# Sums of squares of two weight matrices moved from ScalarE to TensorE, and all low bits of their decoding to ScalarE

## The chip, the cores and the metric

The kernel runs on one core of a Trainium2 chip. The metric is the device time in microseconds. A core has TensorE (PE in the profile; its weight loads are PEld), VectorE (DVE), ScalarE (ACT), GpSimd (POOL) and SyncE (SP), which here only issues DMAs. Every engine works through a queue of its own in order, and engines wait for each other by semaphores.

## The reference

Three parts follow each other: an attention with two softmaxes, a block with a two-dimensional Fourier transform and two large products, and a block with token shift and three products. Inputs are fp32; q, k and v are 8x8x576x64, so that there are 8 batches of 576 tokens with 512 channels.

```python
q_s = softmax(q, axis=-1); k_s = softmax(k, axis=2)
x = q_s @ (k_s.T @ v)                       # per batch and head
mixed = real(fft(fft(x, axis=1), axis=2))
u = x + mixed
un = (u - mean(u)) / sqrt(var(u) + 1e-6)
x = u + relu(un @ w_ch1) @ w_ch2            # 512x2048 and 2048x512
xk, xr = mixes of x with the token before it
out = sigmoid(xr @ w_r) * (relu(xk @ w_k) ** 2 @ w_v)
```

The softmaxes are written here as one word each. The weights of the change are `w_ch1` (w1) and `w_ch2` (w2).

## The kernel before

**Products.** A factor is kept as two fp16 parts, a rounded one and the rest, and a product is three products of parts. The main loop goes over nine blocks of up to 512 tokens. For each block and each of 16 chunks f, `mm1` (L1104) makes 128 hidden channels out of w1, and `mm2` (L1127), two chunks behind, adds their share of w2's result into four banks of PSUM. Between these products `side()` puts the next steps of attention, Fourier transform and norm of later batches, and later the work of the third part, whose products are in L1165, L1218 and L1230.

**The front.** Before the main loop can begin, batch 0 must be through attention, transform and norm, and the weights must be ready. Three generators produce this: `front_x` (attention of each batch: maxima L337 to L349, softmaxes L360 to L376, products L381, transposes L416, results L436), `front_y` (transform: sums and differences L473 to L488, first products L517, second products L537, then the norm with the sums L647) and `front_z` (the weights). `beside_first` takes one step of x or y and, by the rate RATE, 0.4 steps of z, each pinned behind the newest instructions of VectorE and ScalarE. What is left of z follows behind batch 0's norm.

**The weights.** A weight arrives as 32-bit words in pairs, of which the upper word has all but three bits of the value. The 16 chunks of w1 and the 16 of w2 are handled two at a time, in 16 pairs of 128x1024 values, 1 MB of DMA each. Six pairs are loaded ahead; the load of pair k+4 is issued by SP once the high join of pair k has released its buffer (L228, L229). Step k of `front_z` does three things:

- `low_parts(k)`: VectorE shifts the upper words (L168). The low bits are then taken in one of two ways. With `own`, VectorE joins them with a shift (L170). Without it, ScalarE stores them into the low half of the raw upper word (L172), and the next operation brings them along.
- `high_parts(k-1)`: VectorE joins the top bits of pair k-1 (L174), and without `own` the stored low bits too. This waits for L172 of that pair.
- `squares(k-2)`: ScalarE squares all values of pair k-2 and adds them up by row (L234), in an instruction with a read-out of the sum behind it.

`own` is true for even k, so eight pairs go either way. After the last pair of w1 and the last of w2, `scales(w)` adds the eight sums (L243), adds over the partitions with a product by ones (L245), and works out a power of two (L246 to L253). `split(w, c)` then makes the two fp16 parts of each chunk, h on ScalarE (L260) and the rest on VectorE (L261), in place: chunk k is written where chunk k-1 was, so that each split waits for the one before it. The main loop starts with six chunks split, and the other 26 follow beside its first block.

**Warming products.** `warm` (L451) puts products into the front whose result nobody reads, in banks of the tag "h". This tag has two banks, which `mm1` uses later.

The low bits' two ways are in L169 to L172:

```python
if own:
    join(out=x, in0=lo, scalar=29, in1=x, op0=ALU.logical_shift_right, op1=ALU.bitwise_or)
else:
    nc.scalar.activation(out=raw.bitcast(U16)[..., 2], in_=lo, func=AF.Copy, scale=0.9975 * 2.0 ** -29, bias=-0.49)
```

Of the kernel before, what the change touches and what calls it, by code (L numbers as in the profile page):

```python
# [8 lines left out]
F32 = mybir.dt.float32  # L9
F32R = mybir.dt.float32r  # L10
F16 = mybir.dt.float16
BF16 = mybir.dt.bfloat16
U32 = mybir.dt.uint32
U16 = mybir.dt.uint16
AF = mybir.ActivationFunctionType
ALU = mybir.AluOpType
AX = mybir.AxisListType
# [11 lines left out]
POOL_K = ()  # L29
BEHIND_X = {(1, 1): 6}  # L30
RATE = 0.4
OWN = 0
AHEAD_W = 6
FIRST = 1.0
HOLD = {(2, 0): "c"}
# [12 lines left out]
def net(ctx, tc, q, k, v, w1, w2, mu_k, mu_r, w_k, w_v, w_r, ce_d, se_d, cs_d, ss_d, alt_d, id_d, out):  # L48
    nc = tc.nc
# [13 lines left out]
    def bank(tag, bufs, shape=(128, 512)):  # L63
        return ps.tile(list(shape), F32, tag=tag, name=tag, bufs=bufs)
# [3 lines left out]
    def aside(first, strand):  # L68


        turn_of[0] += 1
        if not first:
            return bank(f"side{strand if 'b' in marks or done_block[0] >= 0 else turn_of[0] % 2}", 1)
        x = turn_of[0] % 6
        return bank(f"side{x // 3}", 1) if x in (0, 3) else bank(f"acc{(1, 2, 4, 5).index(x)}", 1)

    mm = nc.tensor.matmul
# [14 lines left out]
    big = main.enter_context(tc.tile_pool(name="big", bufs=1, side="right"))  # L92
# [17 lines left out]
    wr = big.tile([128, len(order) + 1, 512], U32, name="wr", tag="w")  # L110
    wf = wr.bitcast(F16)
    onesr = big.tile([128, 128], F32R, name="onesr")
    ones = onesr.bitcast(F32)
    amax = big.tile([128, 2, 8], F32, name="amax")
    wsc = big.tile([128, 8], F32, name="wsc")

    ident = fc.tile([128, 128], F32, name="ident")
# [45 lines left out]
    def assemble(raw, x, part=None, own=False):  # L163

        hi, lo = raw[..., 1], raw[..., 0]
        join = nc.vector.scalar_tensor_tensor
        if part != 1:
            nc.vector.tensor_scalar(out=x, in0=hi, scalar1=3, scalar2=0x3FFFFFFF, op0=ALU.logical_shift_left, op1=ALU.bitwise_and)  # L168
# [4 lines that stand above are left out]
        if part != 0:  # L173
            join(out=x, in0=hi, scalar=0xC0000000 if own else 0xC0000007, in1=x, op0=ALU.bitwise_and, op1=ALU.bitwise_or)  # L174
# [6 lines left out]
    pairs = [(w, c) for w in range(2) for c in range(0, 16, 2)]  # L181
    raws = {}
# [17 lines left out]
    def load_pair(k):  # L200

        if k >= len(pairs):
            return
        if k == 0:
            raws["places"] = word_places()
        w, c = pairs[k]
        raw = raws[k] = next(raws["places"]).rearrange("p (c n w) -> p c n w", c=2, w=2)
        for x in range(2):
            z = c + x
            if w == 0:  # L210
                src = w1.bitcast(U32)[128 * (z % 4):128 * (z % 4) + 128, 1024 * (z // 4):1024 * (z // 4) + 1024]
            else:
                src = w2.bitcast(U32)[128 * z:128 * z + 128, :]
            nc.sync.dma_start(out=raw[:, x].rearrange("p n w -> p (n w)"), in_=src)

    def words_at(w, c):
        a, b = place[w, c] + 1, place[w, c + 1] + 1
        return wr[:, a:b + 1:b - a]

    def low_parts(k):  # L220

        if k < len(pairs):
            assemble(raws[k], words_at(*pairs[k]), 0, k % 2 == OWN)

    def high_parts(k):
        if 0 <= k < len(pairs):
            assemble(raws.pop(k), words_at(*pairs[k]), 1, k % 2 == OWN)
            if k + 4 >= AHEAD_W:  # L228
                load_pair(k + 4)  # L229

    def squares(w, c):

        dump = wr[:, 0].bitcast(BF16).rearrange("p (c n) -> p c n", c=2)
        nc.scalar.activation(out=dump, in_=words_at(w, c).bitcast(F32), func=AF.Square, accum_out=amax[:, w, c // 2:c // 2 + 1])  # L234

    def scales(w):


        ts = nc.vector.tensor_scalar
        m = wsc[:, 3 * w:3 * w + 1]  # L240
        inv = wsc[:, 3 * w + 1:3 * w + 2]
        mi, ii = m.bitcast(U32), inv.bitcast(U32)
        nc.vector.tensor_reduce(out=m, in_=amax[:, w, :], axis=AX.X, op=ALU.add)  # L243
        pt = aside(False, 0)[:, 0:1]
        mm(out=pt, lhsT=one, rhs=m, start=True, stop=True)  # L245
        ts(out=inv, in0=pt, scalar1=2.0 ** -120, scalar2=None, op0=ALU.max)  # L246
        ts(out=mi, in0=ii, scalar1=1, scalar2=0x3F800000, op0=ALU.logical_shift_right, op1=ALU.bitwise_and)
        ts(out=ii, in0=mi, scalar1=0x7F800000, scalar2=None, op0=ALU.bitwise_xor)

        ts(out=inv, in0=inv, scalar1=(2.0 ** -55, 2.0 ** -51)[w], scalar2=None, op0=ALU.mult)  # L250
        ts(out=m, in0=m, scalar1=(2.0 ** 54, 2.0 ** 50)[w], scalar2=None, op0=ALU.mult)
        if w == 1:
            nc.vector.tensor_tensor(out=wsc[:, 6:7], in0=wsc[:, 0:1], in1=m, op=ALU.mult)  # L253
# [190 lines left out]
    def warm(b, x, src):  # L444

        if b == 0:
            pt = bank("h", 2)
            if len(src.shape) > 2:
                src = src.rearrange(("p a b -> p (a b)", "p a b c -> p (a b c)")[len(src.shape) - 3])
            for _ in range(x):  # L450
                mm(out=pt[:, 0:128], lhsT=ones, rhs=src[:, 0:128], start=True, stop=True)  # L451
# [5 lines left out]
    def transform(b):  # L457
# [11 lines left out]
        if b in (0, 1, 2):  # L469

            for t in range(4):
                for e, op in ((0, ALU.add), (1, ALU.subtract)):
                    tt(out=eo[:, e, t, 1:289], in0=u[:, t, 1:289], in1=u[:, t, S - 1:HALF - 1:-1], op=op)  # L473
                if t == 0 and b == 0:
                    warm(0, 8, eo[:, 0, 0, 1:129])
                if t == 2:
                    nc.scalar.activation(out=x6[0:1, 0:289], in_=eo[0:1, 0, 2, 0:289], func=AF.Copy)
                    tt(out=x6[32:33, 0:289], in0=eo[0:1, 0, 2, 0:289], in1=x6[0:1, 0:289].bitcast(F32), op=ALU.subtract)
                yield 0
            nc.scalar.activation(out=eo[0:1, :, 2, 0:289], in_=eo[0:1, :, 3, 0:289], func=AF.Copy)  # L480
            nc.vector.memset(eo[0:1, 0, 3, 0:289], 0.0)
            for e, op in ((0, ALU.add), (1, ALU.subtract)):
                for g in range(2):
                    tt(out=eo[:, e, g, 0:289], in0=eo[:, e, g, 0:289], in1=eo[:, e, 3 - g, 0:289], op=op)
                    ma = nc.scalar.activation(out=eh[:, e, g, 0:289], in_=eo[:, e, g, 0:289], func=AF.Copy)
                    warm(b, 1, eo[:, e, g, 1:129])
                for g in range(2):
                    mv = tt(out=el[:, e, g, 0:289], in0=eo[:, e, g, 0:289], in1=eh[:, e, g, 0:289].bitcast(F32), op=ALU.subtract)  # L488
# [223 lines left out]
    def last_weights():  # L712
# [35 lines left out]
        def words_of(q):  # L748


            def squares(a, x):
                hw = wp.tile([128, 256], BF16, tag="hw", name="hw", bufs=1)
                nc.scalar.activation(out=hw, in_=x.bitcast(F32), func=AF.Square, accum_out=am[:, q, a:a + 1])

            before = None
            for a, (src, t, c, x) in enumerate(chunks(q)):
                decode(load_weight(wp, src, t, c, RAW), x)
                if before:
                    squares(*before)
                before = a, x  # L760
                yield 0
            squares(*before)
            yield 0
# [200 lines left out]
    def front_z():  # L964
        for k in range(len(pairs) + 2):
            if k < len(pairs):
                low_parts(k)
            high_parts(k - 1)
            if k >= 2:
                squares(*pairs[k - 2])  # L970
            yield 0
            if k - 2 in (7, 15):
                scales((k - 2) // 8)
                yield 0
# [178 lines left out]
    words = big.tile([128, 31, 512], F32, tag="w", name="last")  # L1153
# [221 lines left out]
def build(inputs):  # L1375
    import concourse.bacc as bacc

    nc = bacc.Bacc("TRN2", target_bir_lowering=False, num_devices=1, dynamic_dma_scratch_size=1024)
    arrays, args = {}, []
    for name, a in [*_laid_out(inputs).items(), *_constants().items()]:  # L1380
        arrays[f"in_{name}_dram"] = a
        args.append(nc.dram_tensor(f"in_{name}_dram", a.shape, mybir.dt.from_np(a.dtype), kind="ExternalInput").ap())
    b, _, s, _ = inputs["q"].shape
    args.append(nc.dram_tensor("out_0_dram", (b * s, DM), F32, kind="ExternalOutput").ap())
    with tile.TileContext(nc, schedule_with_timeline_sim=True) as tc:
        net(tc, *args)
    return nc, arrays
# [9 lines left out]
```

## Time and profile before

| | us |
|---|---|
| median of 3 runs | 1457.01 |
| lowest and highest | 1456.41, 1457.19 |
| the profiled execution | 1457.53 |
| its span, first to last instruction | 1455.8 |
| busy: TensorE, its weight loads | 1408.9, 883.1 |
| busy: VectorE, ScalarE, GpSimd | 992.0, 687.4, 26.3 |

The span is shorter than the execution, as the launch and the end lie around it. Busy times are of one profiled execution. Matmuls overlap in TensorE's pipeline and their ends are modelled, so the time that one takes up is better read from the distance between starts than from its duration. The granted clock (PEclk) is the share of 2.4 GHz that TensorE was given; its lower level is 1.2 GHz. A chain of waits is followed back from the last instruction: at each step to what released it, or to the instruction ahead of it on its engine.

### The profile page before, as it was taken

The page shows a single profiled execution, that of the slowest core. Times are in us where ns is not written, and L with a number is a line of the kernel's source. Part 1 is how long each engine was busy: PE and PEld are TensorE (multiplying, and loading weights), DVE is VectorE, ACT ScalarE, POOL GpSimd, SP SyncE. Part 2 cuts the span into 40 slices and gives each one's busy share as a digit, 9 for nine tenths or more (in the row PEclk, how much of TensorE's full clock was granted, in tenths as well). Part 3 has the DMA queues.
Part 4 walks back from the last instruction along what each step waited for, and adds up shares of the span by engine and source line. Part 5 has one row for each costly group of instructions (what it writes and reads, how often), then busy time and mean ns, then how long its engine had stood idle before and what let it go on. Part 6 is the DMA issues. An engine that isn't in the chain of part 4 may idle for free.

```text
span 1455.8 us, 21047 instructions
## 1 busy us (share of the span) xinstructions
PE 1408.9 (97%) x8519; PEld 883.1 (61%) x8519; DVE 992.0 (68%) x1804; ACT 687.4 (47%) x1233; POOL 26.3 (2%) x41
## 2 busy tenths in 40 slices
PE   4679999999999999999999999999999999999998
PEld 3568988886556556556555444445666666666665
DVE  8988686595683774753533476784999788875643
ACT  6776544453342433432322266573766555654422
POOL 1001000000000000000000000000000000000000
PEclk8699999999999999999999999999999999999999
DMA  9830013112011020110011032301011011100001
GB/s 376 297 124 2 18 42 108 54 58 72 17 52 64 27 71 35 52 46 1 0 59 38 15 115 74 116 23 58 30 59 59 22 38 59 52 8 30 29 17 42
DMA packets 38301, 89.47 MB, mean 61 GB/s; under 512 B 5147, under 2 KB 11580, under 8 KB 38204
## 3 DMA queue, kind: packets, MB, share of 16 engines
q1 hardware_dynamic: 37052, 85.30, 16.7%
q0 software_dynamic: 1152, 2.83, 0.6%
q8 instruction: 66, 1.08, 0.3%
q14 instruction: 31, 0.25, 0.1%
HBM read 69.25 MB, written 18.87 MB: 61 GB/s over the span
## 4 chain that ended last, share of the span: by engine, by line
PE 92%; DVE 4%; ACT 2%; issue 1%; DMA 0%; ACTq 0%; DVEq 0%
PE acc L1127 25%; PE h L1104 25%; PE acc L1230 13%; PE h L1165 11%; PE side L1218 6%; PE side L537 2%; PE side L517 2%; PE side L436 2%; PE side L381 1%; PE side L416 1%; DVE wr L174 1%; ACT wr L234 0%; DVE wr L261 0%; PE side L382 0%; ACT u L172 0%
## 5 line engine op out<-in xcount | busy, mean ns | idle before, releaser
L1104 PE MATMUL h<-unh,wr 128*128 128x512 f16 (+1 forms) x1408 | 380.0, 341 | 2.3 <-ACT wr L260 1.4
L1127 PE MATMUL acc<-hh,wr 128*128 128x512 f16 (+1 forms) x1408 | 368.6, 341 | 0.0
L1104 PEld LDWEIGHTS <-wr 128*128 128x128 f16 x2112 | 201.8, 98 | 165.5 <-issue 3.9
L1127 PEld LDWEIGHTS <-wr 128*128 128x128 f16 x2112 | 201.6, 98 | 159.9 <-issue 2.7
L1104 PE MATMUL h<-unl,wr 128*128 128x512 f16 (+1 forms) x704 | 239.3, 341 | 0.0
L1127 PE MATMUL acc<-hl,wr 128*128 128x512 f16 (+1 forms) x704 | 220.0, 341 | 0.0
L1230 PE MATMUL acc<-ring,last 128*128 128x512 f16 x864 | 201.2, 379 | 0.2 <-DVE last L1261 0.2
L1110 DVE SCALAR_TENSOR_TENSOR hl<-h,hh 128x512 f16<-128x512 f32 x144 | 99.1, 688 | 136.0 <-ACT hh L1109 135.2
L1109 ACT ACTIVATE hh<-h 128x512 f16<-128x512 f32 x144 | 85.7, 595 | 170.6 <-PE h L1104 170.1
L1230 PEld LDWEIGHTS <-last 128*128 128x128 f16 x864 | 84.0, 98 | 86.5 <-DVE last L1261 0.7
L1165 PEld LDWEIGHTS <-wkh 128*128 128x128 f16 x1008 | 98.5, 98 | 34.1
L1259 ACT ACTIVATE last<-last,pw 128x512 f32<-128x512 f32 x72 | 51.5, 717 | 106.9 <-DVE last L1258 106.3
L1218 PE MATMUL side<-ring,x 128*128 128x512 f16 x432 | 101.1, 379 | 0.0
L1180 DVE TENSOR_TENSOR last<-h,last 128x512 f32<-128x512 f32 x90 | 61.8, 687 | 49.9 <-PE h L1165 49.8
L1165 PE MATMUL h<-x,wkh 128*128 128x256 f16 x560 | 95.7, 273 | 0.0
L1165 PE MATMUL h<-x,wkl 128*128 128x256 f16 x280 | 76.3, 273 | 0.0
L1165 PE MATMUL h<-last,wkh 128*128 128x256 f16 x448 | 76.1, 273 | 0.0
L1218 PEld LDWEIGHTS <-x 128*128 128x128 f16 x432 | 42.3, 98 | 42.5
L1261 DVE TENSOR_TENSOR last<-last 128x512 f16<-128x512 f32 x72 | 49.5, 687 | 22.1 <-ACT last L1260 21.7
L1165 PE MATMUL h<-last,wkl 128*128 128x256 f16 x224 | 61.1, 273 | 0.0
L894 ACT ACTIVATE aa<-y,ms 128x512 f32<-128x512 f32 x72 | 48.0, 712 | 17.5 <-DVE x L902 12.2
L409 ACT ACTIVATE qT<-side 128x512 fp32r<-128x512 f32 (+3 forms) x44 | 37.0, 840 | 38.3 <-PE side L416 27.7
(358 smaller groups left out, 2087.1 us busy)
## 6 DMA issues: line engine op xcount, KB each, us to landing
vt<-in_v_dram SPq DMA_DIRECT2D x16, 650.0 KB, 5.4
kt<-in_k_dram SPq DMA_DIRECT2D x16, 576.0 KB, 3.9
qt<-in_q_dram SPq DMA_DIRECT2D x16, 576.0 KB, 3.8
out_dram<-oo SPq DMA_DIRECT2D x36, 256.0 KB, 2.0
y<-yT SPq DMA_DIRECT2D x8, 1026.0 KB, 5.3
u<-in_w_dram SPq DMA_DIRECT2D x16, 512.0 KB, 6.2
words<-in_w_dram SPq DMA_DIRECT2D x10, 512.0 KB, 9.9
raw<-in_w_k_dram SPq DMA_DIRECT2D x16, 256.0 KB, 3.6
```

Of the source, the lines that this page charges most:

```text
L409: nc.scalar.activation(out=dst(qT), in_=src, func=AF.Copy)
L894: nc.scalar.activation(out=a, in_=y[:, t, 0:n], func=AF.Copy, scale=mu[:, w, 1, t:t + 1])
L1104: mm(out=pt[:, o:o + m], lhsT=a, rhs=c[:, t, o:o + m], start=(t == z == 0), stop=(t == 3 and z == 2))
L1109: ma = nc.scalar.activation(out=hh[:, 0:n], in_=pt[:, 0:n], func=AF.Relu)
L1110: mv = nc.vector.scalar_tensor_tensor(out=hl[:, 0:n], in0=pt[:, 0:n], scalar=0.0, in1=hh[:, 0:n], op0=ALU.max, op1=ALU.subtract)
L1127: mm(out=acc[x][:, o:o + m], lhsT=a, rhs=c[:, o:o + m], start=(f == z == o == 0), stop=(f == NF - 1 and z == 2), skip_group_check=(i < 2))
L1165: mm(out=pt[:, 256 * x:256 * x + 256], lhsT=c[:, u, 128 * x:128 * x + 128], rhs=d[:, u], start=(fresh and x == u == z == 0), stop=(last an ...
L1180: nc.vector.tensor_tensor(out=out, in0=view(pt), in1=addend, op=ALU.add)
L1218: mm(out=pt, lhsT=a[:, v, u, c, o:o + 128], rhs=w[:, t, :], start=(t == y == 0), stop=(t == 3 and y == 2))
L1230: mm(out=acc[x], lhsT=a[:, 128 * x:128 * x + 128], rhs=c[:, f, :], start=(f == z == 0), stop=(f == 7 and z == 2))
L1259: nc.scalar.activation(out=o, in_=o, func=AF.Square, scale=W["pw"][:, 10 + g:11 + g])
L1261: nc.vector.tensor_tensor(out=l2, in0=o, in1=h2, op=ALU.subtract)
```

## The change

`OWN` becomes empty, so that no pair is `own`: ScalarE stores the low bits of all 16 pairs, and VectorE's low joins in the front are gone. The decoding of the third part's weights doesn't use OWN and stays as it is. `squares` leaves ScalarE: it takes the upper 16 bits of each value as bf16, and for each 128 columns multiplies them on TensorE with themselves, eight products for each pair, adding all 64 of a matrix into a 128x128 corner of one "h" bank. On the diagonal stand the sums of squares of the columns. `scales` multiplies this corner by the identity and adds by row. `warm` keeps one bank, where it took the next of two each time, since the sums hold the other.

```diff
-OWN = 0
+OWN = ()
...
-    amax = big.tile([128, 2, 8], F32, name="amax")
...
-            assemble(raws[k], words_at(*pairs[k]), 0, k % 2 == OWN)
+            assemble(raws[k], words_at(*pairs[k]), 0, k in OWN)
...
-            assemble(raws.pop(k), words_at(*pairs[k]), 1, k % 2 == OWN)
+            assemble(raws.pop(k), words_at(*pairs[k]), 1, k in OWN)
...
     def squares(w, c):
 
-        dump = wr[:, 0].bitcast(BF16).rearrange("p (c n) -> p c n", c=2)
-        nc.scalar.activation(out=dump, in_=words_at(w, c).bitcast(F32), func=AF.Square, accum_out=amax[:, w, c // 2:c // 2 + 1])
+        if "gram" not in raws:
+            raws["gram"] = bank("h", 2)
+        words = words_at(w, c).bitcast(BF16).rearrange("p c (n h) -> p c n h", h=2)[..., 1]
+        for x in range(2):
+            for g in range(0, 512, 128):
+                z = words[:, x, g:g + 128]
+                mm(out=raws["gram"][:, 128 * w:128 * w + 128], lhsT=z, rhs=z, start=(c + x + g == 0), stop=(c + x == 15 and g == 384))
...
-        nc.vector.tensor_reduce(out=m, in_=amax[:, w, :], axis=AX.X, op=ALU.add)
+        dg = wr[:, 0, 128 * w:128 * w + 128].bitcast(F32)
+        nc.vector.tensor_tensor(out=dg, in0=raws["gram"][:, 128 * w:128 * w + 128], in1=ident, op=ALU.mult)
+        nc.vector.tensor_reduce(out=m, in_=dg, axis=AX.X, op=ALU.add)
...
         if b == 0:
-            pt = bank("h", 2)
+            if "idle" not in raws:
+                raws["idle"] = bank("h", 2)
+            pt = raws["idle"]
```

## Rows read from the trace of the kernel before

**Rows 1.** The page's 40 slices of the span: busy tenths, and granted clock (PEclk).

```profile
PE   4679999999999999999999999999999999999998
...
DVE  8988686595683774753533476784999788875643
...
PEclk8699999999999999999999999999999999999999
```

**Rows 2.** Busy us (instructions) by stretch: PE, PEld, DVE, ACT, POOL; clock, DMA share, GB/s.

```profile
17.90:98.10 80.20, 53.86 (x269) 45.25 (x268) 74.48 (x125) 64.29 (x110) 4.71 (x8) 0.77 0.70 262
20.00:45.00 25.00, 14.03 (x53) 11.29 (x54) 24.03 (x38) 22.44 (x41) 4.71 (x8) 0.65 1.07 406
45.00:70.00 25.00, 15.40 (x72) 12.32 (x71) 23.49 (x46) 18.53 (x34) 0.00 (x0) 0.70 0.71 250
70.00:98.00 28.00, 23.60 (x140) 21.07 (x139) 24.79 (x40) 21.35 (x35) 0.00 (x0) 0.91 0.34 133
98.00:130.00 32.00, 27.35 (x225) 22.68 (x223) 30.07 (x53) 19.43 (x34) 4.52 (x2) 1.00 0.17 59
130.00:1452.00 1322.00, 1321.26 (x8003) 809.87 (x8003) 874.31 (x1606) 598.45 (x1084) 16.23 (x24) 1.00 0.13 46
```

**Rows 3.** The chain of waits from 17 to 98 us, by line.

```profile
by line: issue 15.2%; DVE wr L174 9.4%; ACT wr L234 7.8%; ACT u L172 6.6%; ACT words L172 6.2%; DVE wr L168 5.8%; DVE wr L170 5.4%; PE h L451 3.3%; PE side L537 3.2%; ACT qT L409 2.6%; DVE eo L473 2.6%; PE acc L537 2.5%; PE side L647 2.1%; 
```

**Rows 4.** The chain of waits around 40 us: start us, us, what.

```profile
37.44 2.39 ACT words L172
...
39.85 1.23 DVE wr L174
```

**Rows 5.** L170 by stretch: DVE busy us (instructions), clock, DMA share, GB/s.

```profile
17.90:45.00 27.10, 3.65 (x3) 0.67 1.07 407
45.00:70.00 25.00, 3.63 (x3) 0.70 0.71 250
70.00:98.00 28.00, 2.44 (x2) 0.91 0.34 133
```

**Rows 6.** L172 in the whole stretch: ACT busy us (instructions), then as above.

```profile
17.90:98.10 80.20, 20.05 (x8) 0.77 0.70 262
```

**Rows 7.** L234 by stretch: ACT busy us (squares and read-outs), then as above.

```profile
17.90:45.00 27.10, 6.99 (x12) 0.67 1.07 407
45.00:70.00 25.00, 4.64 (x8) 0.70 0.71 250
70.00:98.00 28.00, 6.94 (x12) 0.91 0.34 133
```

**Rows 8.** VectorE's waits from 17.9 to 98.1 us: us in total, times, longest.

```profile
DVE wr L174 <- ACT words L172: 1.3, 2, 0.8
DVE wr L174 <- ACT u L172: 0.8, 1, 0.8
```

**Rows 9.** Lines L243, L706, L709: ns min/median/max, first and last start us.

```profile
L243 DVE TENSOR_REDUCE wsc<-amax x2: 144/149/154, 58.2 to 95.1; 128x1 f32<-128x8 f32 x2
...
L706 DVE TENSOR_TENSOR dg<-ident,z x2: 281/283/285, 938.2 to 976.7; 128x128 f32<-128x128 f32 x2
...
L709 DVE TENSOR_REDUCE z<-side x2: 280/286/291, 942.9 to 1012.3; 128x1 f32<-128x128 f32 x2
```

**Rows 10.** The chain of waits from 66 to 98 us: start us, us, what.

```profile
69.48 2.06 PE acc L537 x7
...
72.50 1.45 PE side L537 x6
...
90.54 1.34 PE h L451 x12
```

**Rows 11.** Busy us by stretch of one clock, columns as in rows 2.

```profile
68.70:75.20 6.50, 5.72 (x24) 5.72 (x25) 5.04 (x10) 5.42 (x7) 0.00 (x0) 0.51 1.01 395
75.40:98.00 22.60, 18.20 (x117) 15.66 (x116) 20.99 (x35) 17.02 (x29) 0.00 (x0) 1.00 0.18 70
```

**Rows 12.** Line L260, ScalarE's part of the splits: ns min/median/max, first and last start us.

```profile
L260 ACT ACTIVATE wr<-wr,wsc x32: 705/722/724, 96.6 to 163.6; 128x512 f16<-128x512 f32 x32
```

## The prediction

> **What bounds the kernel now.** I start with the page's 40 slices [rows 1]. From the fourth slice on TensorE reads 9 to the end; in the first three it reads 4, 6 and 7 at granted clocks of 0.8, 0.6 and 0.9, while VectorE reads 8, 9 and 8. So the kernel has two parts: a front that TensorE doesn't fill, and a long remainder that it does. The same by stretches in us [rows 2]: from 130 to 1452 us TensorE is busy 1321.26 of 1322 us, so work saved there on any other engine is worth nothing, while an earlier begin of this part moves the end by as much. From 17.9 to 98.1 us, where the weights are decoded, VectorE is busy 74.48 of 80.20 us (93%), ScalarE 64.29 (80%), TensorE 53.86 (67%). All eight removed joins and all 16 squares lie in this stretch, so the change is priced there. From 98 to 130 VectorE still leads with 30.07 of 32 us, and TensorE waits 4.65 us in sum; a gain of the front is passed on through it, as the work that VectorE does there begins earlier.
>
> Third, the chain of waits of that stretch by line [rows 3]: the high joins L174 hold 9.4% of it, the squares L234 7.8%, the low stores L172 12.8% (6.6 and 6.2), L168 5.8%, the low joins L170 5.4%. No engine owns it. Last, the chain's pieces around 40 us [rows 4]: a low store of 2.39 us, and then the high join that waited for it. There ScalarE leads, not VectorE.
>
> **The change, part by part.** Durations are of the profiled execution, 1457.53 us, which is 0.5 us above the median of the three runs (1457.01).
>
> *Low joins gone from VectorE.* Eight of them, 9.72 us in all, 3.65 before 45 us, 3.63 from 45 to 70 and 2.44 from 70 to 98 [rows 5].
>
> *Low stores added on ScalarE.* The same eight pairs now get L172, whose eight instances took 20.05 us, 2.5 us each [rows 6]: 20.05 us more.
>
> *Squares gone from ScalarE.* 16 with their read-outs, 18.57 us: 6.99, 4.64 and 6.94 in the three stretches [rows 7]. So ScalarE's work hardly changes (+1.5 us), but it moves forward: a store stands at the head of a pair's work, a square two steps behind it. Pairs 0, 2 and 4 add 7.5 us before 45 us, pairs 6, 8 and 10 add 7.5 between 45 and 70, pairs 12 and 14 add 5.0 after it. With the loads of [rows 2], and the little from 17.9 to 20 us counted in, ScalarE comes to 22.4 + 7.5 - 7.0 = 22.9 of 25 us, 18.5 + 7.5 - 4.6 = 21.4 of 25, and 21.35 + 5.0 - 6.9 = 19.4 of 28. VectorE comes to 20.4, 19.9 and 22.4.
>
> *A new wait.* Each high join now waits for a store, where half did. In this stretch VectorE waited 2.1 us for stores (1.3 and 0.8) [rows 8]. Behind a waiting L174 stands everything that attention and transform have queued on VectorE. From below nothing is added, since a store issued one step ahead may be done; from above another 2.1 us. It lies inside the densities used below, and I count it in the range only.
>
> *The scales.* Each of two reductions of 8 columns (149 ns) becomes a product with the identity (283 ns) and a reduction of 128 columns (286 ns) [rows 9]: +0.42 us each, +0.84 us on VectorE, the second just ahead of the splits.
>
> *Products on TensorE.* 16 pairs of 8, 128 in all, each 128x128 with a weight load of its own. No row has this shape in bf16. The nearest are fp32 products of the same shape at full clock: 12 in 1.34 us, 0.112 us each [rows 10]. At half clock I double it, 0.22 us, just under the 0.242 us of a 290-column product at half clock (six in 1.45 us) [rows 10]. The stretch was granted 0.77 on the mean, which is 54% of its time at 2.4 GHz and the rest at 1.2: 0.54 x 0.112 + 0.46 x 0.22 = 0.16 us, an estimate, and 20.7 us for all. TensorE idles 80.2 - 53.9 = 26.3 us here, so the lower end on the path is nothing, and the upper end is all 20.7 us. Nobody waits for a sum until the scales, so they cost only what they hold up on TensorE's own queue. TensorE's shown lines are 11.1% of the chain (L451 3.3, L537 5.7, L647 2.1) [rows 3]; I take that share, 2.3 us.
>
> The Trainium skill, page "TensorE: Matmul & The Clock Gate", section "Back-to-back issue gap", gives about 81 ns for a sustained pair of load and 128-column product. By it the sum would be 10.4 us instead of 20.7, and 1.2 us on the path instead of 2.3; the rows here never show such a pair.
>
> *Clock.* From 68.7 to 75.2 us the grant was 0.51, though TensorE was busy 5.72 of 6.5 us; from 75.4 it is 1.00 [rows 11]. The transform's second products (L537) run in just that piece, seven and six of them on the chain from 69.48 us on [rows 10]. At full clock the 5.7 us would be 2.9. More products ahead of it may hold the clock up or not: 0 to -2.9, I take -1.3.
>
> *Loads and banks.* SP issues a pair's load when the high join of the pair four before it has released the buffer; it keeps its place behind that join, and no DMA is added. The DMA engines are full up to 45 us (share 1.07) and at 0.71 behind it [rows 2]: before 45 us an earlier join can't bring an earlier landing, a second reason to expect little there. The two h banks hold the sums and the warming products; the main loop's first product wants the first of them, but also a split, which the program puts behind both scales, so this costs nothing.
>
> *Sum.* The densest that VectorE gets today is 24.03 and 23.49 of 25 us [rows 2], some 95%, and I give ScalarE the same. 17.9 to 45 us: ScalarE's 22.9 us by 0.95 are 24.1 of 25: I take -0.5. 45 to 70: 21.4 by 0.95 are 22.5: -2.5. 70 to 98: VectorE's -2.4 with +0.84: -1.6. Products +2.3, clock -1.3. Together -3.6: 1457.5 - 3.6 = 1453.9 in the profiled execution, 1453.4 as a median.
>
> **The rivals.** *ScalarE takes over, no change.* By the chain's own shares [rows 3], times 81 us: L170's 5.4% is 4.4 us gone, L234's 7.8% is 6.3 us gone, and eight more stores at the share of the eight that are there (12.8%) bring 10.4 us back. Net -0.3; with products, clock and scales (2.3 - 1.3 + 0.4) it is +1.1: 1458.1 as a median. For it speaks that a store heads the chain in [rows 4]; against it that ScalarE had 6.5 us idle from 45 to 70 and 6.6 after.
>
> *Slower: TensorE's queue.* Place: the products of a pair stand in program order ahead of attention's and the transform's, and wait for the pair's high join. If they hold these up by half of their 20.7 us, that is 10.4 us against 5.9 (4.6 of the stages and 1.3 of the clock): +4.5, 1461.5 as a median. It decides from 8.8 us on the path on (5.9 + 2.9). For it: TensorE would be busy 53.9 + 20.7 of 80.2 us. Against it: it idles in every stretch today, and the products' data are two steps old.
>
> *The whole gain of VectorE.* -9.72 + 0.84 = -8.9 us where VectorE stays the only bound, -2.9 from the clock, and +1.2 of products (half of the 2.3 above): 1457.5 - 10.6, 1446.4 as a median. For it: 93% busy today. Against it: 22.9 of 25 us on ScalarE in the first stretch. The same page of the Trainium skill, "What's actually happening", says that activity releases the throttle, which favours the clock term; [rows 11] agree only in part, as a nearly full engine ran at 0.51.
>
> **How the numbers follow.** A measurement of this kernel tells about 0.2%, 2.9 us, from no change. My forecast has 0.42, the whole gain 0.10: faster 0.52. ScalarE taking over has 0.31: same. TensorE's queue has 0.17: slower. The range runs from the whole gain, 1446, to just short of the slower case, 1461; beyond it lie half of that case and a little of the whole gain. The forecast's own range, with the store waits of 2.1 us and the products between 0 and 4 us, is 1449 to 1456.
>
> **What would show it.** In the profile after: no L170 in the front, 16 stores of 2.5 us, no Square in the front, 128 products. Right, if VectorE's busy time from 18 us to the first split falls by some 9 us and that split starts 3 to 5 us before its 96.6 [rows 12], with the remainder unchanged. If VectorE's waits for stores grow to 6 us or more, ScalarE took over. If L436, L517 or L537 start late behind the new products, TensorE's queue did. If TensorE's clock is 1.00 by 60 us, the clock term was too small. I'd be wrong altogether if the part behind 130 us changed its length by over 2 us.

## The result, and the profile after

The median of four runs is 1468.60 us (1468.13 to 1470.20), against 1456.71 us (1456.18 to 1457.19) of the kernel before on the same chip: ratio 1.0083, 95% interval 1.0067 to 1.0099. The change makes the kernel slower by 11.9 us, outside the predicted range. The profiled execution of after took 1470.20 us, its span 1468.4.

The edit moves the line numbers: the shift is L167 in after (before L168), the low store L171 (L172), the high join L173 (L174), the products L238, the splits on ScalarE L266 (L260), `mm1` L1112 (L1104).

The page's slices of after, as in [rows 1]:

```profile
PE   4589999999999999999999999999999999999998
...
DVE  6788666587584674863533466784999788876643
```

VectorE's first slices read 6, 7 and 8 instead of 8, 9 and 8. The engine that was busiest in the front is less busy, and yet the front is longer. The windows of after, columns as in [rows 2], show it by stretch:

```profile
17.90:98.10 80.20, 54.04 (x350) 46.18 (x350) 60.29 (x104) 59.06 (x76) 4.85 (x8) 0.81 0.71 262
20.00:45.00 25.00, 13.18 (x73) 10.56 (x74) 15.76 (x24) 22.78 (x32) 4.85 (x8) 0.68 1.04 381
45.00:70.00 25.00, 15.67 (x108) 13.75 (x107) 20.37 (x40) 14.42 (x24) 0.00 (x0) 0.77 0.50 183
70.00:98.00 28.00, 23.50 (x165) 20.42 (x163) 22.09 (x39) 20.46 (x21) 0.00 (x0) 0.94 0.60 217
```

From 17.9 to 98.1 us VectorE is busy 60.29 us, where it was 74.48 [rows 2]; ScalarE, too, is less busy than before (59.06 against 64.29). No engine is the bound of this stretch by its busy time. What filled it instead is in VectorE's waits from 17.9 to 110 us (us in total, times, longest), the view of [rows 8]:

```profile
DVE wr L173 <- ACT u L171: 10.4, 7, 2.5
DVE wr L173 <- ACT words L171: 5.8, 5, 2.9
DVE wr L173 <- ACT raw L171: 3.2, 3, 2.6
```

The high joins waited 19.4 us in sum for ScalarE's low stores, in 15 of 16 pairs; before it was 2.1 us [rows 8]. In the chain of waits from 17 to 98 us the stores now hold 31.3%, where they held 12.8 [rows 3]:

```profile
by line: issue 20.9%; ACT u L171 12.7%; ACT words L171 10.3%; ACT raw L171 8.3%; DVE wr L167 7.1%; DMA words<-in_w_dram 6.6%; ACT qT L415 5.2%; DVE wr L173 5.1%; PE acc L545 3.6%; DVE eo L492 1.7%; DVE qt L382 1.6%; DVE el L496 1.6%; DVE d 
```

One pair in full, VectorE's timeline of after (start us, us, what, idle time before it and what ended it):

```profile
64.80 0.68 DVE L167 TENSOR_SCALAR wr<-raw 128x1024 uint32<-128x1024 uint32 x1
68.07 1.22 DVE L173 SCALAR_TENSOR_TENSOR wr<-raw,wr 128x1024 uint32<-128x1024 uint32 x1 [2.58 <-ACT raw L171]
69.21 0.69 DVE L167 TENSOR_SCALAR wr<-words 128x1024 uint32<-128x1024 uint32 x1
```

and ScalarE's in the same stretch:

```profile
65.52 2.52 ACT L171 ACTIVATE raw<-raw 128x1024 uint16<-128x1024 uint32 x1 [1.65 <-DVE wr L167]
```

The store takes the raw words when the shift has read them, and the join stands right behind its own shift in VectorE's queue: VectorE idles for one whole store. The next pair's shift, which the program text puts ahead of this join, stands behind it: the order in a queue is worked out by a planner, and it isn't that of the text. The Trainium skill, page "TensorE: Matmul & The Clock Gate", section "Architectural detail: the array is 16× 32×32, not 1× 128×128", says that the queues of ScalarE and VectorE are strictly first in, first out; the trace agrees, as the shift of 69.21 us did not pass the waiting join. Taken from the end of the shift to the start of the join, ten of the 16 pairs lie between 2.54 and 2.60 us, one store each, whether VectorE filled that time with other work or not.

In the kernel before, the same stretch of VectorE's timeline:

```profile
67.15 0.69 DVE L168 TENSOR_SCALAR wr<-u 128x1024 uint32<-128x1024 uint32 x1
67.75 1.22 DVE L174 SCALAR_TENSOR_TENSOR wr<-u,wr 128x1024 uint32<-128x1024 uint32 x1
...
70.25 0.68 DVE L168 TENSOR_SCALAR wr<-raw 128x1024 uint32<-128x1024 uint32 x1
70.85 1.22 DVE L174 SCALAR_TENSOR_TENSOR wr<-u,wr 128x1024 uint32<-128x1024 uint32 x1
71.98 1.22 DVE L170 SCALAR_TENSOR_TENSOR wr<-raw,wr 128x1024 uint32<-128x1024 uint32 x1
```

The shift of 67.15 us belongs to a stored pair, whose join is the one of 70.85. Between them stand the join of the pair before, steps of the scales and of the transform, and the shift of the next pair, 3 us of work that covers the store; neither join shows an idle time. The join of the pair before is one with `own`, so it waits for no store. Such a join stands between shift and join in seven of the eight stored pairs; a removed low join (L170) stands there in none. By the two timelines, VectorE has 3.1 us of work on the mean between the shift and the join of a stored pair before, and 1.8 us after, less than one store. What covered the stores was the order of VectorE's queue, with the high joins of the `own` pairs in it, and not the work that the change removes.

Where the 12.6 us of span lie (1468.4 against 1455.8) is read from the splits and from `mm1` (ns min/median/max, first and last start us), after:

```profile
L266 ACT ACTIVATE wr<-wr,wsc x32: 704/722/723, 107.3 to 172.8; 128x512 f16<-128x512 f32 x32
...
L1112 PE MATMUL h<-unh,wr x1408: 272/379/421, 108.1 to 1008.0; 128*128 128x512 f16 x112, 128*128 128x256 f16 x64
```

and `mm1` before:

```profile
L1104 PE MATMUL h<-unh,wr x1408: 269/379/392, 98.1 to 995.3; 128*128 128x512 f16 x112, 128*128 128x256 f16 x64
```

The first split begins 10.7 us later than in [rows 12], `mm1` 10.0 us later. From its first to its last start it takes 899.9 us instead of 897.2, +2.7, and behind it nothing changes (460.4 against 460.5). So the front costs 10 us and the main loop 2.7. For VectorE the two fronts, each up to its first split, are these windows, before and then after (columns as in [rows 2]):

```profile
17.90:96.60 78.70, 52.36 (x256) 43.76 (x255) 73.26 (x121) 62.79 (x106) 4.71 (x8) 0.76 0.71 267
...
17.90:107.30 89.40, 61.34 (x399) 52.46 (x398) 67.32 (x119) 65.79 (x85) 4.85 (x8) 0.81 0.64 235
```

VectorE's busy time falls by 5.9 us and its idle time rises by 16.6, together the 10.7. Its waits for stores alone are 17.3 us more. The busy time falls by less than the 8.9 us that the change takes off (9.72 less 0.84), as 2.9 us of other steps now stand ahead of the split.

### The profile page after: what moved, and what is told of

It reads as the page before. It is cut to its first block, busy times and chain, and to the rows that moved or that the text cites. A ratio compares the mean times of both kernels' runs of the same rounds, so it can differ in the third digit from the quotient of the medians.

```text
span 1468.4 us, 21260 instructions
## 1 busy us (share of the span) xinstructions
PE 1417.9 (97%) x8647; PEld 891.7 (61%) x8647; DVE 983.6 (67%) x1798; ACT 689.7 (47%) x1209; POOL 26.4 (2%) x41
## 4 chain that ended last, share of the span: by engine, by line
PE 90%; DVE 4%; ACT 3%; issue 1%; DMA 1%; POOL 0%; SPq 0%; ACTq 0%; DVEq 0%; POOLq 0%
PE h L1112 25%; PE acc L1135 24%; PE acc L1238 13%; PE h L1173 11%; PE side L1226 6%; PE side L525 2%; PE side L545 2%; PE side L442 2%; PE side L387 2%; DMA kt<-in_k_dram 1%; ACT u L171 1%; PE side L422 1%; ACT words L171 1%; ACT raw L171 0%; PE side L388 0%
## 5 line engine op out<-in xcount | busy, mean ns | idle before, releaser
L1112 PE MATMUL h<-unh,wr 128*128 128x512 f16 (+1 forms) x1408 | 380.5, 341 | 3.5 <-DVE wr L267 2.1
L1112 PEld LDWEIGHTS <-wr 128*128 128x128 f16 x2112 | 202.6, 98 | 167.5 <-issue 3.0
L1112 PE MATMUL h<-unl,wr 128*128 128x512 f16 (+1 forms) x704 | 239.8, 341 | 0.5 <-DVE unl L691 0.5
L902 ACT ACTIVATE aa<-y,ms 128x512 f32<-128x512 f32 x72 | 48.0, 711 | 17.4 <-DVE x L910 12.2
L1173 PEld LDWEIGHTS <-wkl 128*128 128x128 f16 x504 | 49.3, 98 | 6.4
```

The lines of the kernel that those rows point to most:

```text
L902: nc.scalar.activation(out=a, in_=y[:, t, 0:n], func=AF.Copy, scale=mu[:, w, 1, t:t + 1])
L1112: mm(out=pt[:, o:o + m], lhsT=a, rhs=c[:, t, o:o + m], start=(t == z == 0), stop=(t == 3 and z == 2))
L1173: mm(out=pt[:, 256 * x:256 * x + 256], lhsT=c[:, u, 128 * x:128 * x + 128], rhs=d[:, u], start=(fresh and x == u == z == 0), stop=(last an ...
```

## The experiments

Theory A: the joins' waits for stores are the loss. Theory B: the products are, through TensorE's queue. A third (A2 in the expectations): it is ScalarE's load. Every run has its own runs of the kernel before beside it, 1456.6 to 1456.9 us. A time called "one run" has no interval; repeats of one kernel here spread by up to 3.6 us.

**Squares alone moved.** Of the changed kernel, with every second pair `own` again:

```diff
-OWN = ()
+OWN = (0, 2, 4, 6, 8, 10, 12, 14)
```

> The sums of squares stay on TensorE, the low bits of the even pairs go back to VectorE. Theory A (the high joins wait on VectorE for ScalarE's stores): their waits, 19.4 us between 18 and 110 us in the changed kernel, fall below 4 us, the first split starts at 96 us or earlier instead of 107.3, and the time is 1450 to 1457 us. Theory B (the 128 products hold up attention and transform in TensorE's queue): all products are still there, so the time stays at 1465 to 1470 us.

1460.98 us, ratio 1.0030 (1.0017 to 1.0043), between the ranges of A and of B. The joins waited 3.5 us, and the first split began at 97.9. The window of 17.9 to 98.1 us:

```profile
17.90:98.10 80.20, 54.59 (x395) 47.29 (x393) 74.73 (x124) 47.98 (x77) 4.69 (x8) 0.89 0.69 260
```

ScalarE is rid of 16 us of work, and this buys nothing, as VectorE has as much to do as before (74.73 against 74.48). So 7.6 of the 11.9 us go with the stores, and the products with what comes with them cost 4.1, which A had not expected.

**Stores alone moved**, squares left on ScalarE, no product at all. Of the kernel before:

```diff
-OWN = 0
+OWN = 2
```

> The kernel before with the low bits of all 16 pairs stored by ScalarE, and its squares kept on ScalarE; no products. Theory A: the waits of the high joins are at least the 19.4 us of the changed kernel, and ScalarE has some 20 us more to do than before: 1470 to 1485 us. Theory B: without the products the time is that of before, 1455 to 1459 us.

One run: 1467.81 us. VectorE's waits from 17.9 to 110 us:

```profile
DVE wr L174 <- ACT words L172: 8.1, 5, 3.3
DVE wr L174 <- ACT u L172: 7.2, 6, 1.8
DVE wr L174 <- ACT raw L172: 2.2, 3, 1.3
DVE wr L174 <- ACT seh L136: 2.0, 1, 2.0
```

19.5 us of waits at the joins, `mm1` from 107.0: almost the whole loss without a product, against theory B, though 2 us short of what A gave. The two parts (11.0 us here, 4.1 for the products above) don't add up to the 11.9, as both moves change the same queues.

**Products two steps later**, so that none stands at the head of TensorE's queue for a fresh pair:

```diff
-        for k in range(len(pairs) + 2):
+        for k in range(len(pairs) + 4):
...
-            if k >= 2:
-                squares(*pairs[k - 2])
+            if k >= 4:
+                squares(*pairs[k - 4])
...
-            if k - 2 in (7, 15):
-                scales((k - 2) // 8)
+            if k - 4 in (7, 15):
+                scales((k - 4) // 8)
```

> The changed kernel with each pair's products emitted two steps later, four behind its shift. Theory A: TensorE's idle time before the products falls, VectorE's waits for stores stay near 19 us, and the time stays within 2 us of 1468.6. Theory B: products whose data are there hold nothing up, and the time falls by 6 us or more, to 1462 us or less.

One run: 1470.49 us. TensorE's wait ahead of the products fell from 12.9 us to 8.8, the waits for stores stayed (9.3, 6.9 and 2.8, 19.0 in sum), and the time didn't fall. Theory B falls.

**Half a store.** Only 512 of 1024 columns of each pair are stored (the low bits of the others are left out), 1.35 us each:

```diff
-                nc.scalar.activation(out=raw.bitcast(U16)[..., 2], in_=lo, func=AF.Copy, scale=0.9975 * 2.0 ** -29, bias=-0.49)
+                st, si = (raw[:, 0:1].bitcast(U16), lo[:, 0:1]) if len(raw.shape) > 3 else (raw.bitcast(U16), lo)
+                nc.scalar.activation(out=st[..., 2], in_=si, func=AF.Copy, scale=0.9975 * 2.0 ** -29, bias=-0.49)
```

> The changed kernel with each of the 16 stores cut to half its columns (the low three bits of the other half are left as they come): 1.3 us a store instead of 2.5. Theory A: with the stores half as long the waits of the high joins fall to 8 us or less and the time to 1454 to 1462 us. Theory B: the products are as before, 1465 to 1470 us.

One run: 1456.74 us, joins' waits for stores 5.9 us, first split 96.1: the loss is gone with half of the store's length. But ScalarE's load fell as well.

**No wait.** The stores go to a spare place which the joins don't read (the low bits are left out):

```diff
-                nc.scalar.activation(out=raw.bitcast(U16)[..., 2], in_=lo, func=AF.Copy, scale=0.9975 * 2.0 ** -29, bias=-0.49)
+                spot = raw.bitcast(U16)[..., 2] if len(raw.shape) == 3 else wr[:, 0].bitcast(U16).rearrange("p (c n) -> p c n", c=2)
+                nc.scalar.activation(out=spot, in_=lo, func=AF.Copy, scale=0.9975 * 2.0 ** -29, bias=-0.49)
...
-        dg = wr[:, 0, 128 * w:128 * w + 128].bitcast(F32)
+        dg = raws["gram"][:, 128 * w:128 * w + 128]
```

> The changed kernel with the 16 stores of the front kept on ScalarE, but written to a spare place that the high joins don't read (the low three bits of w1 and w2 are left as they come; the product with the identity is written into the sums' own bank). ScalarE keeps its work, VectorE and TensorE theirs; only the wait of the join for the store is gone. Theory A (the wait is the cost): VectorE's waits at the high joins are under 1 us, the first split starts at 96 us or earlier, and the time is 1448 to 1457 us. Theory A2 (ScalarE's load is the cost, as the stores hold attention's and the transform's own steps up): the first split stays behind 102 us, and the time at 1463 us or more.

One run: 1450.72 us, no waits of the joins, first split at 82.9. It proves less than was meant. The line of its stores:

```profile
L172 ACT ACTIVATE wr<-u x8: 1126/1144/1178, 23.2 to 80.6; 128x1024 uint16<-128x1024 uint32 x8
```

With the 16-bit results side by side, a store took 1.14 us instead of 2.5. ScalarE lost some 22 us of work, which the expectation had not foreseen, and wait and load fell together. A later run parts them.

**All pairs own.** No store in front of the main loop at all:

```diff
-OWN = ()
+OWN = tuple(range(16))
```

> The changed kernel with all 16 low joins on VectorE and no store: VectorE gets 19.5 us of joins where the changed kernel has none and waits 19.4 us for stores, ScalarE loses 40 us. Theory A: no waits at the high joins; VectorE is the bound with 9.7 us more than before and close to no idle time, so the first split starts 5 to 10 us later than before, and the time is 1462 to 1468 us. Theory A2: with ScalarE unloaded the front is shorter than before, 1456 us or less.

One run: 1468.94 us, 0.9 us above the expectation and as slow as the change, for the opposite reason. No wait for a store, but

```profile
17.90:98.10 80.20, 58.64 (x362) 49.53 (x361) 78.99 (x123) 26.52 (x62) 5.12 (x8) 0.74 0.70 261
```

VectorE is busy 78.99 of 80.20 us; ScalarE's 26.52 don't help. ScalarE's load is not the bound here.

**Twelve stores**, four pairs own:

```diff
-OWN = ()
+OWN = (0, 4, 8, 12)
```

> The changed kernel with four low joins back on VectorE (pairs 0, 4, 8 and 12), twelve stores. Theory A: it lies between the 1461.0 us of eight stores and the 1468.6 of sixteen, with waits at the high joins near 10 us: 1462 to 1467 us.

One run: 1460.81 us, a little under the expectation; waits 9.2 us (5.6 and 3.6), first split 99.2. With 0, 8, 12 and 16 stores and the squares on TensorE the times are 1468.9, 1461.0, 1460.8 and 1468.6: VectorE's work at one end, its waits at the other.

**The join a step later.** High joins of pair k-2 in step k, products one step behind:

```diff
-            high_parts(k - 1)
-            if k >= 2:
-                squares(*pairs[k - 2])
+            high_parts(k - 2)
+            if k >= 3:
+                squares(*pairs[k - 3])
...
-            if k - 2 in (7, 15):
-                scales((k - 2) // 8)
+            if k - 3 in (7, 15):
+                scales((k - 3) // 8)
```

> The changed kernel with each high join emitted one step later, two behind its shift, and the products one step later too; the loads that wait for a join move with it. Theory A: what counts is the work that stands between shift and join in VectorE's queue. In the queue as it is written out the joins of ten pairs or so still stand within a few instructions of their shifts, so the waits fall from 19.4 us by a third at most, and the time to 1462 to 1468 us. Theory A2: no change beyond 2 us of 1468.6.

One run: 1466.59 us. A later place in the text took off only a third of the waits (8.7, 3.0 and 0.6 left, 12.3 in sum), since the queue's order isn't the text's, and others came: 4.7 us at `rk` of the attention.

**The join pinned behind the next pair's shift.** All of the change's work is kept; only the place in VectorE's queue is fixed:

```diff
+    shifts = []
...
-            nc.vector.tensor_scalar(out=x, in0=hi, scalar1=3, scalar2=0x3FFFFFFF, op0=ALU.logical_shift_left, op1=ALU.bitwise_and)
+            shifts.append(nc.vector.tensor_scalar(out=x, in0=hi, scalar1=3, scalar2=0x3FFFFFFF, op0=ALU.logical_shift_left, op1=ALU.bitwise_and))
...
-            assemble(raws.pop(k), words_at(*pairs[k]), 1, k in OWN)
+            with behind_one(shifts[k + 1] if k + 1 < len(pairs) else None):
+                assemble(raws.pop(k), words_at(*pairs[k]), 1, k in OWN)
```

> The changed kernel, all its work kept, with each high join pinned in VectorE's queue behind the shift of the next pair, so that the work between two shifts covers the store. Theory A (the wait, through the place of the join in the queue, is the cost): waits at the high joins fall from 19.4 us to under 6, the first split starts before 100 us, and the time is 1450 to 1459 us. Theory A3 (it isn't the place: the stores are late because ScalarE is late with them wherever the join stands, and the join then only waits later or holds the loads up): 1464 us or more.

1460.08 us, ratio 1.0023 (1.0013 to 1.0033): 8.5 us won back with nothing but order, though 1.1 us above theory A's range; the first split begins at 100.0 us. With the pin VectorE has 3.7 us of work on the mean between a pair's shift and its join. VectorE's waits from 17.9 to 110 us:

```profile
DVE wr L175 <- ACT u L173: 3.5, 4, 1.7
DVE rk L393 <- PE acc L391: 3.5, 1, 3.5
...
DVE wr L175 <- ACT words L173: 0.9, 2, 0.5
DVE wr L175 <- ACT raw L173: 0.7, 1, 0.7
```

5.1 us of store waits are left, and 3.5 at `rk`. The latter is what the early stores do to the attention on ScalarE's own queue. It shows at the second exponential of batch 0's keys. In ScalarE's timeline of the kernel before:

```profile
35.06 1.18 ACT L370 ACTIVATE kt<-kt 128x1152 f32<-128x1152 f32 x1
```

In that of this run:

```profile
39.00 1.17 ACT L379 ACTIVATE kt<-kt 128x1152 f32<-128x1152 f32 x1
```

Behind the early stores it starts 3.9 us later (and at 41.12 us in after, which has the waits as well).

**The join pinned two shifts behind**, on top of the join a step later:

```diff
-            with behind_one(shifts[k + 1] if k + 1 < len(pairs) else None):
+            with behind_one(shifts[k + 2] if k + 2 < len(pairs) else None):
```

> The same with each join one step later and pinned behind the shift of the second pair after its own. Theory A: hardly any wait at the joins; but the load that each join releases comes later by a pair, so shifts may wait for loads: 1450 to 1462 us. Theory A3: 1464 us or more.

1468.35 us, ratio 1.0079 (1.0064 to 1.0094): a miss. VectorE's waits:

```profile
DVE rk L393 <- PE acc L391: 7.1, 1, 7.1
DVE wsc L358 <- PE acc L356: 3.0, 1, 3.0
...
DVE wr L169 <- DMA u<-in_w_dram: 2.0, 2, 1.6
```

The joins wait 0.3 us for stores in all, but attention is no earlier (this `rk` at 44.93 us, 44.33 in the run before), and, as a join also frees the buffer for a load, the shifts now wait for loads. More distance than the wait needs made it worse.

**Early pairs own, late ones pinned.** Pairs 0, 2 and 4 `own`, joins pinned from pair 5 on:

```diff
-OWN = ()
+OWN = (0, 2, 4)
...
-            with behind_one(shifts[k + 1] if k + 1 < len(pairs) else None):
+            with behind_one(shifts[k + 1] if 5 <= k < len(pairs) - 1 else None):
```

> The pinned kernel (each high join behind the shift of the next pair) with the low joins of pairs 0, 2 and 4 back on VectorE, so that ScalarE has three stores before 45 us, as before the change, and all stores after; the pins start at pair 5. Theory A: attention's second exponential, at 35.1 us before the change, 41.1 after it and 39.0 with pins alone, is back at 36 us or earlier, waits at the high joins stay under 6 us, VectorE is spared five joins (6.1 us), and the time is 1451 to 1458 us. Theory A3 (late stores are the cost wherever the join stands): 1460 us or more.

1456.54 us, ratio 0.9997 (0.9988 to 1.0006): the whole loss is gone. The exponential in ScalarE's timeline of this run:

```profile
31.65 1.22 ACT L379 ACTIVATE kt<-kt 128x1152 f32<-128x1152 f32 x1
```

With three early stores fewer it starts ahead of before's 35.06 us; the store waits are 2.4 us, the first split begins at 96.2. It doesn't beat the kernel before.

**One product in eight.** The first run, squares alone, with only the first 128 columns of each pair squared (the others are left out of the sums):

```diff
-        for x in range(2):
-            for g in range(0, 512, 128):
-                z = words[:, x, g:g + 128]
-                mm(out=raws["gram"][:, 128 * w:128 * w + 128], lhsT=z, rhs=z, start=(c + x + g == 0), stop=(c + x == 15 and g == 384))
+        z = words[:, 0, 0:128]
+        mm(out=raws["gram"][:, 128 * w:128 * w + 128], lhsT=z, rhs=z, start=(c == 0), stop=(c == 14))
```

> The kernel with half the low bits on each engine (squares only moved, 1461.0 us) with one product for each pair instead of eight: 16 products, which sum an eighth of the squares. If the 128 products' time in TensorE's queue is what made that kernel 4.1 us slower than before, it comes back to 1456 to 1458 us or below, as ScalarE is spared its squares. If it is something else that came with them (the products' place in the queue and their wait for the join, the longer scales, the order at the main loop's begin), it stays at 1459.5 to 1462 us.

1459.00 us, ratio 1.0016 (1.0006 to 1.0025): 2.0 us less than with all products, between the two expectations. The first split begins at 95.2 us, ahead of before, yet `mm1` takes 902.6 us from first to last start, in an execution 1.7 us above this run's median. The front gains, and in this execution the main loop gives back: TensorE waits 2.1 us for VectorE ahead of 333.6 us, and from 334.4 to 337.8 us it is granted 0.51.

**The store beside the join's half.** This parts wait and load. The stores keep their 8-byte stride but go into the low word's own half, which the joins don't read:

```diff
-                nc.scalar.activation(out=raw.bitcast(U16)[..., 2], in_=lo, func=AF.Copy, scale=0.9975 * 2.0 ** -29, bias=-0.49)
+                spot = raw.bitcast(U16)[..., 0 if len(raw.shape) > 3 else 2]
+                nc.scalar.activation(out=spot, in_=lo, func=AF.Copy, scale=0.9975 * 2.0 ** -29, bias=-0.49)
```

> The changed kernel with its 16 stores in front of the main loop written into the low word's own half (the same 8-byte stride, so about 2.5 us each again) instead of the half that the high join reads; the join then takes the low bits from nobody (the three low bits of the decoded words are not the reference's in these pairs). ScalarE keeps all of its 16 stores at their old length, only the wait is gone. Theory A (the joins' waits for stores are the loss): no wait of the joins for ScalarE, VectorE busy about 72 to 76 us of 17.9 to 98.1, first split 90 to 99 us, time 1453 to 1459. Rival A2 (ScalarE's load itself, late for the attention and for the loads of the next pairs, which still wait for the store, is the loss, and the 1.14 us stores of the earlier run without waits were what gained): first split 103 us or later, time 1464 or more.

1455.18 us, ratio 0.9986 (0.9976 to 0.9995). The stores that read `u`, by line (ns min/median/max, first and last start us):

```profile
L172 ACT ACTIVATE u<-u x8: 2505/2523/2613, 24.7 to 86.8; 128x1024 uint16<-128x1024 uint32 x8
```

The window of 17.9 to 98.1 us:

```profile
17.90:98.10 80.20, 57.80 (x405) 50.37 (x404) 70.64 (x128) 66.32 (x89) 5.05 (x8) 0.85 0.70 262
```

The splits on ScalarE:

```profile
L267 ACT ACTIVATE wr<-wr,wsc x32: 706/722/732, 93.6 to 159.6; 128x512 f16<-128x512 f32 x32
```

All 16 stores at 2.5 us, ScalarE busier than in after (66.32 against 59.06), all 128 products: and without the wait the time is 13.4 us lower, the first split 13.7 us earlier. ScalarE's load and the products together don't cost the kernel its 11.9 us; the handover with its waits does. Time and split are within what theory A expected (VectorE's 70.64 us are not, it gave 72 to 76), and A2 falls. The edit takes both waits of the handover away, as a store that leaves the upper word alone doesn't wait for the shift that reads it either (ScalarE's waits for shifts were 12.1 us in after). The pinned run keeps both, and shows that the join's place alone is worth 8.5 us.

## Why the prediction was wrong

**The step that failed** is "A new wait". It put the added wait for stores between nothing and another 2.1 us, "since a store issued one step ahead may be done", and counted it in the range only. The runs show 17.3 us more (19.4 against 2.1). The lower bound took the join to stand a step behind its shift, as in the text; in the queue of after it stands one store behind in ten of 16 pairs, with 1.8 us of work between on the mean. The upper bound was the present wait once more, eight stores like the eight before; but the present wait of 2.1 us was measured where each stored pair stood between two own ones, whose high joins wait for no store, and with 3.1 us of work between. The rows to bound it by were at hand: the store's 2.5 us [rows 6] times 16 pairs is 40 us, less what else VectorE finds to do between a shift and its join. The pieces of [rows 4], a store of 2.39 us and then its join, already showed a join that waited, by 0.85 us in VectorE's timeline; VectorE had filled the rest of that store with other work, so "ScalarE leads" was true of those 0.85 us only.

**The densities** hung on this. The sum let VectorE and ScalarE each fill 95% of the stages of 25 us. After, VectorE filled 15.76 and 20.37, ScalarE 22.78 and 14.42: where each waits for the other in turn, a store for its shift and a join for its store, neither is dense. The three stage terms (-0.5, -2.5, -1.6) became +10.7 us in front of the first split. In the run without the wait, the first split began 3.0 us earlier than before, inside the "3 to 5 us before its 96.6" that the prediction gave, and the time was 1.5 us lower where the sum had 3.6. That run is rid of the old 2.1 us of waits as well. So the other terms together had the right sign, and came to less than half of their size.

**Products.** The estimate of 0.16 us each, 20.7 us in all, was too high. L238 in after, busy us and count on TensorE and its weight loads, clock, DMA share, GB/s:

```profile
17.90:108.00 90.10, 12.18 (x128) 9.76 (x128) 0.81 0.64 234
```

From TensorE's timeline of after, one pair's eight at a granted clock of 1.00 and one at 0.50:

```profile
36.19 0.63 PE L238 MATMUL h<-wr 128*128 128x128 bf16 x8 [1.32 <-DVE wr L173]
40.57 1.03 PE L238 MATMUL h<-wr 128*128 128x128 bf16 x8 [3.75 <-DVE wr L173]
```

All 128 are busy 12.2 us. A single one takes 0.217 us at least and 0.330 at most, by the line of these products (ns min/median/max, first and last start us):

```profile
L238 PE MATMUL h<-wr x128: 217/218/330, 23.6 to 103.9; 128*128 128x128 bf16 x128
```

With 0.22 us taken off at full clock and 0.33 at half, seven more take 0.41 and 0.70 us: 0.059 and 0.10 us each, as an estimate. Most starts within such a group lie 0.057 and 0.107 us apart. fp32 products of the same shape, at 0.112, were not a near row. The 81 ns that the prediction quoted from the Trainium skill, page "TensorE: Matmul & The Clock Gate", section "Back-to-back issue gap", don't hold here at either clock; the 55.8 ns, an estimate by the same section's formula for a lone product of 128 columns at full clock, lie near the 0.059. What the products cost the path, +2.3 in the sum, has one measure: in the kernel with eight stores, seven in eight of them gone are worth 2.0 us.

**TensorE's queue**, the rival of the other sign, had the sign right and the cause wrong: moving the products away from the head changed nothing, and the loss came without products. In after TensorE does wait 12.9 us ahead of them, but for the high joins, which are late themselves.

**ScalarE takes over** was nearest in its mechanism. Its test ("VectorE's waits for stores grow to 6 us or more") is met threefold. But it priced the eight added stores by the chain's share of the eight that were there, 10.4 us, and took 6.3 us off for the squares. ScalarE wasn't the bound, so the test doesn't tell its own rival from a wait that the queue's order makes: rid of the squares alone, nothing was won; and the stores' share didn't double with their number, it went from 12.8% to 31.3%.

**The whole gain of VectorE** fell with the same wait. Without it, VectorE's 11.0 us (9.72 less 0.84, and the 2.1 us of old waits) brought 3.0 us at the first split. In that run's chain of waits from 17 to 94 us the stores still hold the most of all lines, 24.1%:

```profile
by line: issue 16.4%; ACT u L172 12.8%; ACT words L172 11.3%; PE acc L388 4.2%; PE acc L526 4.2%; ACT qT L416 4.1%; DVE eo L482 3.6%; ACT kt L377 2.9%; ACT qt L370 2.9%; ACT yh L533 2.5%; PE h L460 2.2%; PE side L526 2.0%; ACT u L444 1.7%; 
```

So ScalarE's load doesn't make the loss, but without the wait it seems to be what keeps the gain small: the one run with stores of 1.14 us began its splits another 10.7 us earlier (82.9) and took 4.5 us less.

**Clock.** The stretch of 45 to 70 us was granted 0.77 instead of 0.70, 70 to 98 us 0.94 instead of 0.91, in the direction of the term; what it was worth no run parts from the rest. Not foreseen: pieces at half clock around the main loop's begin. Two windows of after, columns as in [rows 2]:

```profile
104.00:108.00 4.00, 3.62 (x18) 3.25 (x16) 4.00 (x10) 1.79 (x4) 0.00 (x0) 0.57 0.00 0
...
118.00:122.00 4.00, 4.00 (x23) 3.04 (x22) 2.44 (x5) 2.38 (x4) 0.00 (x0) 0.60 0.42 124
```

Before, 1.00 was granted from 75.4 us on [rows 11], [rows 2]. The prediction wanted "the remainder unchanged", and it grew by 2.7 us, more than the 2 us that it named as a sign of being wrong altogether. These pieces are hardly the cause: the pinned run had one of them (0.63 over four us) and an `mm1` of 896.6 us. TensorE's waits from 150 to 1009 us show where the time went; before has none there, after has these two:

```profile
PE side L442 <- DVE qTl L417: 1.5, 1, 1.5
PE side L610 <- DVE sq L629: 1.1, 1, 1.1
```

Together they are 2.6 us, waits for VectorE's steps beside the loop. In the five profiles with at most 0.2 us of such waits `mm1` takes 896.6 to 898.5 us, in the ten others 897.6 to 902.6. Why VectorE is late there stays open.

## What to carry to other kernels

When a handover between two engines is doubled in number, price the wait by the producer's duration less the work that stands between producer and consumer in the consumer's queue, and look whether that work will wait itself after the change; the wait measured in the old layout is no bound. An engine that is 93% busy doesn't speed up by losing 12% of its work if more of what is left has to wait for another engine. And where the order in a queue is made by a planner, a consumer gets its distance by a pin to one named instruction, not by a later place in the text; more distance than the wait needs delays what hangs on the consumer.

## What the runs showed of the hardware

ScalarE's store of 128x1024 32-bit values as 16-bit ones took 2.5 us with its results 8 bytes apart and 1.14 us with them side by side, the input's stride being the same. The long ones wrote into the tile that they read, the short ones into another; no run parts that from the spacing. Products of 128x128 in bf16, with a weight load of their own each and operands taken 4 bytes apart (the upper halves of 32-bit words), mostly started 0.057 us after each other at full clock and 0.107 at half, in groups of eight.
